# Linear attention and two feed-forward layers on one core: blocks of 512, 512, 256, 512, 512 tokens in the later passes, with one buffer for x's split

## The chip, the cores and the metric

One core of a Trainium2 chip runs the whole program. The metric is the device time of one execution in microseconds (us). The engines are called as in the profile: PE is TensorE (PEld its weight loads), DVE is VectorE, ACT is ScalarE, POOL is GpSimd, SP the engine that issues the DMAs. A matmul streams the columns of one operand through another that a weight load has put in place before; "width" below is the number of streamed columns.

## What is computed

The reference, cut to what matters (4 x 576 = 2304 tokens, 8 heads of 64, model width 512, inner width 2048, all float32):

```python
def _attn_ref(q, k, v):                       # softmax of q over its 64, of k over the 576 tokens
    kv = np.einsum('bhsd,bhse->bhde', k_s, v)
    return np.einsum('bhsd,bhde->bhse', q_s, kv)
def _moe_ref(x, w_in, w_out):                 # first layer: SiLU
    h = x @ w_in
    return (h * (1.0 / (1.0 + np.exp(-h)))) @ w_out
def _moe2_ref(x, w_in, w_out):                # second layer: Mish
    h = x @ w_in
    return (h * np.tanh(log1p(exp(h)))) @ w_out
out = _moe2_ref(_moe_ref(attention as 2304 x 512))
```

## The kernel before

**Passes, blocks, chunks.** The inner width of 2048 is cut into 16 chunks of 128. Each layer is done in two passes of 8 chunks, since the weights of 8 chunks (pool `wres`) are what is kept at a time; `passes` (L124) has four of them, two of the SiLU layer and two of the Mish layer. A pass goes over the 2304 tokens in six blocks of 384 (`BLK`, `NB`). For a block and a chunk there are two products: G1 (`ev_g1`, L645) multiplies the chunk's 512 x 128 piece of w_in by x, 12 matmuls; the activation, and a split of its result into a rounded part and a rest, give g; G2 (`ev_g2`, L664) multiplies g by the chunk's piece of w_out and adds to four banks of PSUM over the 8 chunks. Float32 accuracy comes from three products of rounded parts and rests (w, x and g each lie as two float32r parts), which is why G1 has 4 x 3 matmuls. In the SiLU layer w is the loaded and g the streamed operand of G2: 12 matmuls as wide as the block. In the Mish layer g is loaded, 128 tokens at a time, and w is streamed, 512 columns: 9 matmuls for a block of 384, however the tokens are cut three for each 128.

**What sets the order.** The list `events` (L125) has for each block X, then G1 of chunks 0 to 3, G2 of chunk 0, G1 of chunk 4, G2 of chunk 1 and so on (`SKEW` = 3 chunks apart), G2 of the last four chunks, and E. X (`ev_x`, L635) makes x's two parts, four copies on ACT and four subtractions on DVE into the tile `xs`; E (`ev_e`, L681) moves the sums out of PSUM. The first pass also carries the attention; in it a scheduler places the steps by priority. Once attention and the first weights are done, in the last-but-one block of the first pass, the loop at L745 closes the pools of the first part, opens others in their place (L746 to L752), and from there on each engine issues in the order in which the code is written (`InOrder`, L34; such instructions have line L49 in the profile, the others L47). From then on X is written `X_LEAD` = 7 events ahead of its place (L756) and a second buffer for `xs` alternates with the first (L638). If the switch happens with fewer than 7 events to go, X is written at its own place, behind E.

**Weights.** For each piece a DMA brings 64-bit words into a staging tile `st` (three of them after the switch), `w_take` and `w_join` decode them into `wt`, `w_high` and `w_low` split that into the two parts of `w`. `w_plan` (L216) sets the places in `events` where this is done. The DMA for the piece three further on waits until the join has read its staging tile.

Of the kernel before, what the change touches and what calls it, by code (L numbers as in the profile page):

```python
# [55 lines left out]
def attention_silu_mish(ctx: ExitStack, tc: tile.TileContext, q, k, v, w_in1, w_out1, w_in2, w_out2, out):  # L56
# [14 lines left out]

    BLK = 384
    NB = NT // BLK
    NT2 = BLK // P
    HALF = NCH // 2

    PARTS = (((0, HALF), (HALF, NCH)),) * 2
# [2 lines left out]


    X_LEAD, W_LEAD, T_LAG, P_LAG, A_END = 7, 8.0, 3.0, 4.0, 8.0


    W_EVERY, W_WAIT = 4.0, 8
# [11 lines left out]
    const = ctx.enter_context(tc.tile_pool(name="const", bufs=1))  # L97
    wres = ctx.enter_context(tc.tile_pool(name="wres", bufs=HALF))
    xp = ctx.enter_context(tc.tile_pool(name="xp", bufs=1))
    gp = ctx.enter_context(tc.tile_pool(name="gp", bufs=2))  # L100
    gr = ctx.enter_context(tc.tile_pool(name="gr", bufs=SKEW + 1))
    pp = ctx.enter_context(tc.tile_pool(name="pp", bufs=1, space=PSUM))

    ident = const.tile([P, P], F32, name="ident")
# [17 lines left out]


    passes = [(L, c0, c1) for L in range(2) for c0, c1 in PARTS[L]]  # L124
    events, need = [], []  # L125
    for p, (L, c0, c1) in enumerate(passes):
        cs = list(range(c0, c1))
        pend = []
        for j in range(NB):
            events.append(("X", p, j, 0))  # L130
            for c in cs:
                events.append(("G1", p, j, c))
                pend.append(("G2", p, j, c))
                if len(pend) > SKEW:
                    events.append(pend.pop(0))
            events.extend(pend)
            pend = []
            events.append(("E", p, j, 0))
        need += [e for e in events if e[0] in ("G1", "G2") and e[1] == p and e[2] == 0]
# [76 lines left out]
    def w_plan(start):  # L216
        first_mish = next(i for i, e in enumerate(events) if e[1] == len(PARTS[0]))
        ends, taken, split = [], start, 0.0
        for n in range(N0, len(need)):
            kind, p, _, c = need[n]  # L220
            last = max(i for i, e in enumerate(events) if e == (kind, p - 1, NB - 1, c - HALF if c >= HALF else c + HALF))
            if n % N0 == 0:
                taken = max(taken, nat[("X", p - 1, 1, 0)])
            b = max(taken, ends[-W_WAIT] + 0.5 if len(ends) >= W_WAIT else 0.0)
            taken = b + (W_EVERY if b < last - 8 else 2.0)
            s = max(last + 0.5, b + 2.0, split + 1.0)
            split = s
            ends.append(s + 1.0)
            assert s + 3.0 < nat[need[n]], (n, s, nat[need[n]])
            signed = b < first_mish - 1  # L230
            box = {}
            for k, f in ((b, w_take), (b + 1.0, w_join), (s, w_high), (s + 1.0, w_low)):
                todo.setdefault(int(k), []).append((k, f, n, signed, box))
# [32 lines left out]


    l1 = ExitStack()
    pools["st"] = l1.enter_context(tc.tile_pool(name="wst", bufs=4))
    pools["tm"] = l1.enter_context(tc.tile_pool(name="wtm", bufs=3))  # L270
    qp_ = l1.enter_context(tc.tile_pool(name="qp", bufs=4))
# [214 lines left out]
    def attn_start():  # L486

        n = BLK
        rn = n // P
        kt, qt, va = {}, {}, {}  # L490
        for hp in range(NP):
            kt[hp] = load_k(0, hp)
        for hp in range(NP):
            qt[hp] = load_q(0, 0, hp, 0, P, rn)
        for hp in range(NP):
            va[hp] = load_v(0, hp)
        xs[(0, 0)] = x = xp.tile([P, KC, 2, BLK], F32R, tag="xs", name="xs")
        qn = [room(P, 2 * rn * D) for _ in range(NP)]
        st = {}

        def step(what, hp):
            def do(f, *args):
                st[what, hp] = f(*args)

            def got(what):
                return st[what, hp]

            if what == "A":
                do(kT_turn, kt[hp])
            elif what == "M":  # L510
                do(kT_max, got("A"))
            elif what == "B":
                do(kT_exp, got("A"), got("M"), hp)
            elif what == "Z":
                do(kT_sum, got("B")[1])
            elif what == "K":
                do(ke_turn, got("B")[0])
            elif what == "C":
                do(ke_copy, got("K"), kt[hp])
            elif what == "D":  # L520
                do(kv_prod, kt[hp], va[hp])
            elif what == "F":
                kvs[(0, hp)] = kv_scale(got("D"), got("Z"))
            elif what == "Q":
                do(q_max, qt[hp])
            elif what == "S":
                do(q_sub, qt[hp], got("Q"))
            elif what == "E":
                do(q_exp, qt[hp])
            elif what == "R":  # L530
                do(q_sum, qt[hp])
            elif what == "N":
                do(q_norm, qt[hp], got("R"), qn[hp])
            elif what == "T":
                do(q_turn, got("N"))
            elif what == "U":
                do(q_copy, got("T"), later(xa, hp, BLK, P, BLK))
            elif what == "X":
                do(x_prod, got("U"), kvs[(0, hp)])
            elif what == "H":  # L540
                S.copy(tokens(x[:, hp, 0], rn), queries(got("X"), rn))
            elif what == "L":
                V.tensor_tensor(
                    out=tokens(x[:, hp, 1], rn), in0=queries(got("X"), rn), in1=tokens(x[:, hp, 0].bitcast(F32), rn), op=ALU.subtract
                )
            elif what == "P":
                warm_up(hp)
            elif what == "Y":
                InOrder.on = False
                tc.cur_priority += 1000  # L550
                S.copy(tokens(xaT[:, hp, :BLK], rn), queries(got("X"), rn))
                InOrder.on = True

        InOrder.on = True
        for i, o in enumerate(START):
            tc.cur_priority = 400 + 10 * i
            step(o[0], int(o[1]))
        InOrder.on = False
# [75 lines left out]

    def ev_x(p, j):  # L635
        src = xaT if passes[p][0] == 0 else xbT
        ts = slice(j * BLK, (j + 1) * BLK)
        pool = pools["xs"] if "xs" in pools and j % 2 else xp  # L638
        t = pool.tile([P, KC, 2, BLK], F32R, tag="xs", name="xs")
        for kc in range(KC):  # L640
            S.copy(t[:, kc, 0], src[:, kc, ts])
            V.tensor_tensor(out=t[:, kc, 1], in0=src[:, kc, ts], in1=t[:, kc, 0].bitcast(F32), op=ALU.subtract)
# [2 lines left out]
    def ev_g1(p, j, c):  # L645
        L = passes[p][0]
        w = w_get("G1", p, c)
        x = xs[(p, j)]
        h = banks("h1", (4, 5) if L == 0 else (4, 5, 6, 7))[:, :BLK]

        steps = [(kc, i) for i in range(3) for kc in range(KC)]
        if (p, j) == (0, 0) and c < 2:
# [1 line left out]
        for n, (kc, i) in enumerate(steps):  # L654
            s = slice(kc * P, (kc + 1) * P)
            T.matmul(h, w[:, i // 2, s], x[:, kc, i % 2], start=(n == 0), stop=(n == len(steps) - 1))
        g = gr.tile([P, 2, BLK], F32R, tag="g", name="g")
        gf = gp.tile([P, BLK], F32, tag="gf", name="gf")
        S.activation(out=gf, in_=h, func=ACTF.Silu if L == 0 else ACTF.Mish)
        V.tensor_copy(g[:, 0], gf)  # L660
        V.tensor_tensor(out=g[:, 1], in0=gf, in1=g[:, 0].bitcast(F32), op=ALU.subtract)
# [2 lines left out]
    def ev_g2(p, j, c, tiles=None):  # L664
# [1 line left out]
        w = w_get("G2", p, c)  # L666
        g = gt[(p, j, c)]
        if c == c0:
            acc[(p, j)] = [banks("acc", (0, 1, 2, 3)) for _ in range(KC if L == 0 else NT2)]
        st, sp = (c == c0), (c == c1 - 1)  # L670
        for n, (iw, ig) in enumerate(((0, 0), (0, 1), (1, 0))):
            for i, a in enumerate(acc[(p, j)]):
# [1 line left out]
                    continue  # L674
                s = slice(i * P, (i + 1) * P)
                if L == 0:
                    T.matmul(a[:, :BLK], w[:, iw, s], g[:, ig], start=st and n == 0, stop=sp and n == 2)
                else:
                    T.matmul(a, g[:, ig, s], w[:, iw], start=st and n == 0, stop=sp and n == 2)

    def ev_e(p, j, tiles=None):  # L681
        L, c0, c1 = passes[p]
        for i, a in enumerate(acc[(p, j)]):
            if tiles is not None and i not in tiles:
                continue
            if L == 0:
                y = xbT[:, i, j * BLK:(j + 1) * BLK]
                if c0:
                    V.tensor_tensor(out=y, in0=a[:, :BLK], in1=y, op=ALU.add)
                elif i % 2:  # L690
                    V.tensor_copy(y, a[:, :BLK])
                else:
                    S.copy(y, a[:, :BLK])
            else:
                it = j * NT2 + i
                o = xaO[:, it]
                if c0:
                    V.tensor_tensor(out=o, in0=a, in1=o, op=ALU.add)
# [44 lines left out]
            order.pop(0)  # L743

    for i, (what, p, j, c) in enumerate(events):  # L745
        if "xs" not in pools and state["dec"] == N0 and not order and i >= xat[1] + PACE[1] * steps["rest"] + A_END:  # L746
            w_late()
            l1.close()
            for nm, nb in (("st", 3), ("tm", W_WAIT), ("xs", 1)):
                pools[nm] = ctx.enter_context(tc.tile_pool(name="l" + nm, bufs=nb, reuse_waits="tile"))  # L750
            w_plan(i + 0.5)
            InOrder.on = True  # L752
        for k, f, *args in sorted(todo.pop(i - 1, []), key=lambda a: a[0]):
            at(k)
            f(*args)
        if InOrder.on and i + X_LEAD < len(events) and events[i + X_LEAD][0] == "X":  # L756
            at(i)
            ev_x(*events[i + X_LEAD][1:3])
        if what == "X":
            if p == 0:  # L760
                while order and order[0] <= j:
# [6 lines left out]
        if i >= len(events) - SKEW - 2:  # L768
            if what == "G2":
                tail.append(c)  # L770
                continue
            for n in range(NT2):
                for c in tail:
                    ev_g2(p, j, c, (n,))
                ev_e(p, j, (n,))
# [41 lines left out]
```

## Time and profile before

| | |
|---|---|
| median of 3 runs | 887.65 us (887.1 to 887.94) |
| profiled execution, its own time | 888.09 us |
| its span in the trace | 886.3 us |
| granted TensorE clock, mean | 0.999 |
| PE busy | 869.8 us, 98% |
| DVE busy | 444.6 us, 50% |
| ACT busy | 303.1 us, 34% |

The span is the time from the first to the last instruction of the program in the trace; 1.8 us of the execution lie around it. Busy times of matmuls overlap, since a matmul starts before the one ahead of it has ended; the time a stream of matmuls takes is read from the starts. "1.76 ... x4" means that four instructions in a row took 1.76 us together. The granted clock is a share of 2.4 GHz.

### The profile page before, as it was taken

The numbers are of one execution on the slowest core, as the hardware profiler recorded it, in microseconds if no ns is written. First come the engines' busy times: TensorE is split into PE (matmuls) and PEld (weight loads), VectorE is DVE, ScalarE is ACT, GpSimd is POOL, SyncE is SP. The second block draws the span as 40 slices with busy tenths as digits, with TensorE's granted clock in tenths as the row PEclk, the third lists the DMA queues.
The fourth block names the chain that finished last, engine by engine and source line by source line (L and its number), as shares of the span: only waits on it lengthen the run. The fifth ranks groups of instructions, "written<-read, shape, count | busy, mean of one in ns | idle before, by whom it ended". The sixth has DMA issues, their size and how long they took to land.

```text
span 886.3 us, 12434 instructions
## 1 busy us (share of the span) xinstructions
PE 869.8 (98%) x5002; PEld 810.4 (91%) x5002; DVE 444.6 (50%) x965; ACT 303.1 (34%) x592; POOL 54.0 (6%) x82
## 2 busy tenths in 40 slices
PE   7899999999999999999999999999999999999998
PEld 6688988999989999999999998998998998998997
DVE  5999366762366634523358435522349433333332
ACT  5987254563245412211235222312245211211210
POOL 3145011231000000000000000000000000000000
PEclk9999999999999999999999999999999999999999
DMA  9996211310044312200004011200002000000000
GB/s 233 248 241 131 65 36 36 72 37 1 3 140 143 96 48 64 60 21 1 1 25 143 25 47 55 65 24 1 1 24 95 1 36 37 1 36 36 1 36 36
DMA packets 61913, 53.23 MB, mean 60 GB/s; under 512 B 30368, under 2 KB 55456, under 8 KB 61856
## 3 DMA queue, kind: packets, MB, share of 16 engines
q1 hardware_dynamic: 61856, 52.44, 21.4%
q8 instruction: 39, 0.64, 0.3%
q14 instruction: 18, 0.15, 0.1%
HBM read 47.71 MB, written 4.72 MB: 59 GB/s over the span
## 4 chain that ended last, share of the span: by engine, by line
PE 72%; DVE 0%; ACT 0%; issue 0%
PE psum L49 72%; DVE xa L49 0%; ACT xs L49 0%
## 5 line engine op out<-in xcount | busy, mean ns | idle before, releaser
L49 PE MATMUL psum<-xs,w 128*128 128x384 f32 x1836 | 336.5, 335 | 0.9 <-ACT xs L49 0.8
L49 PEld LDWEIGHTS psum<-xs,w 128*128 128x128 f32 x1836 | 321.9, 188 | 7.4 <-ACT xs L49 1.8
L49 ACT ACTIVATE gf<-psum 128x384 f32<-128x384 f32 x153 | 74.9, 490 | 405.4 <-PE psum L49 316.2
L49 PE MATMUL psum<-w,g 128*128 128x512 f32 x864 | 208.0, 392 | 0.0
L49 PEld LDWEIGHTS psum<-w,g 128*128 128x128 f32 x864 | 161.3, 188 | 31.0
L49 DVE CAST g<-gf 128x384 fp32r<-128x384 f32 x153 | 55.0, 359 | 242.8 <-ACT gf L49 242.7
L49 PE MATMUL psum<-g,w 128*128 128x384 f32 x720 | 130.6, 334 | 0.0
L49 PEld LDWEIGHTS psum<-g,w 128*128 128x128 f32 x720 | 125.3, 188 | 0.0
L47 PE MATMUL psum<-xs,w 128*128 128x384 f32 x468 | 98.3, 350 | 3.0 <-ACT gf L47 1.9
L49 DVE TENSOR_TENSOR g<-gf,g 128x384 fp32r<-128x384 f32 x153 | 85.5, 559 | 5.3
L47 PEld LDWEIGHTS psum<-xs,w 128*128 128x128 f32 x468 | 80.2, 189 | 7.2 <-ACT gf L47 2.8
L47 PE MATMUL psum<-g,w 128*128 128x384 f32 x432 | 84.8, 343 | 1.2 <-DVE g L47 1.2
L47 PEld LDWEIGHTS psum<-g,w 128*128 128x128 f32 x432 | 74.7, 188 | 2.6 <-DVE g L47 1.7
L49 ACT CAST w<-wt 128x512 fp32r<-128x512 f32 x48 | 29.6, 617 | 20.9 <-DVE wt L49 15.4
L47 DVE CAST g<-gf 128x384 fp32r<-128x384 f32 x39 | 16.3, 419 | 38.8 <-ACT gf L47 38.5
L47 ACT ACTIVATE gf<-psum 128x384 f32<-128x384 f32 x39 | 18.9, 490 | 41.0 <-PE psum L47 36.9
L49 DVE TENSOR_TENSOR w<-wt,w 128x512 fp32r<-128x512 f32 x48 | 32.6, 685 | 0.6 <-ACT w L49 0.3
L49 ACT ACTIVATE wt<-st 128x512 f32<-128x512 f32 x48 | 31.8, 672 | 0.0
L49 DVE TENSOR_TENSOR xa<-psum,xa 128x512 f32<-128x512 f32 x18 | 11.5, 686 | 36.4 <-PE psum L49 36.4
L47 ACT ACT_TABLE_LOAD x22 | 28.2, 1283 | 4.3 <-PE psum L47 2.3
L49 DVE TENSOR_TENSOR xb<-psum,xb 128x384 f32<-128x384 f32 x24 | 11.7, 550 | 30.6 <-PE psum L49 30.6
L47 DVE TENSOR_TENSOR g<-gf,g 128x384 fp32r<-128x384 f32 x39 | 25.0, 641 | 1.0
(108 smaller groups left out, 561.1 us busy)
## 6 DMA issues: line engine op xcount, KB each, us to landing
st<-in_moe_w_in_dram SPq DMA_DIRECT2D x32, 512.0 KB, 3.9
st<-in_moe_w_out_dram SPq DMA_DIRECT2D x32, 512.0 KB, 3.5
out_dram<-xa SPq DMA_DIRECT2D x18, 256.0 KB, 2.1
xb<-in_k_dram SPq DMA_DIRECT2D x16, 144.0 KB, 3.4
xb<-in_v_dram SPq DMA_DIRECT2D x8, 288.0 KB, 6.8
xa<-in_k_dram SPq DMA_DIRECT2D x16, 144.0 KB, 6.2
xb<-in_v_dram SPq DMA_DIRECT2D x16, 144.0 KB, 3.6
qt<-in_q_dram SPq DMA_DIRECT2D x8, 192.0 KB, 3.3
```

The costliest lines, as they stand in the source:

```text
L47: return call(*args, **kwargs)
L49: self.last = call(*args, **kwargs)
```

## The change

The first pass keeps its six blocks of 384. The three others get five blocks, 512, 512, 256, 512 and 512 tokens wide (`WIDE`), each with its own tile sizes. There is one buffer for `xs` at a time, in a pool of its own that is closed and opened again at the switch, as are now those of `g` and `gf`, and X is written `X_NEAR` = 5 events ahead of its place, which is right behind the last G1 of the block before. The core of the diff:

```diff
-    NT2 = BLK // P
+    NARROW = [(j * BLK, BLK) for j in range(NB)]
+    WIDE = [(0, 512), (512, 512), (1024, 256), (1280, 512), (1792, 512)]
...
+    X_NEAR = SKEW + 2
...
-    gp = ctx.enter_context(tc.tile_pool(name="gp", bufs=2))
-    gr = ctx.enter_context(tc.tile_pool(name="gr", bufs=SKEW + 1))
...
+    blocks = [NARROW] + [WIDE] * (len(passes) - 1)
...
-        for j in range(NB):
+        for j in range(len(blocks[p])):
...
+    pools["xs"] = l1.enter_context(tc.tile_pool(name="xs", bufs=1))
+    pools["gf"] = l1.enter_context(tc.tile_pool(name="gp", bufs=2))
+    pools["g"] = l1.enter_context(tc.tile_pool(name="gr", bufs=SKEW + 1))
...
-        ts = slice(j * BLK, (j + 1) * BLK)
-        pool = pools["xs"] if "xs" in pools and j % 2 else xp
-        t = pool.tile([P, KC, 2, BLK], F32R, tag="xs", name="xs")
+        t0, n = blocks[p][j]
+        ts = slice(t0, t0 + n)
+        t = pools["xs"].tile([P, KC, 2, n], F32R, tag="xs", name="xs")
...
-        h = banks("h1", (4, 5) if L == 0 else (4, 5, 6, 7))[:, :BLK]
+        h = banks("h1", (4, 5) if L == 0 else (4, 5, 6, 7))[:, :blocks[p][j][1]]
...
-            acc[(p, j)] = [banks("acc", (0, 1, 2, 3)) for _ in range(KC if L == 0 else NT2)]
+            acc[(p, j)] = [banks("acc", (0, 1, 2, 3)) for _ in range(KC if L == 0 else blocks[p][j][1] // P)]
...
-        if "xs" not in pools and state["dec"] == N0 and not order and i >= xat[1] + PACE[1] * steps["rest"] + A_END:
+        if not InOrder.on and state["dec"] == N0 and not order and i >= xat[1] + PACE[1] * steps["rest"] + A_END:
...
-            for nm, nb in (("st", 3), ("tm", W_WAIT), ("xs", 1)):
+            for nm, nb in (("xs", 1), ("gf", 2), ("g", SKEW + 1), ("st", 3), ("tm", W_WAIT)):
...
-        if InOrder.on and i + X_LEAD < len(events) and events[i + X_LEAD][0] == "X":
+        if InOrder.on and i + X_NEAR < len(events) and events[i + X_NEAR][0] == "X":
             at(i)
-            ev_x(*events[i + X_LEAD][1:3])
+            ev_x(*events[i + X_NEAR][1:3])
```

What it does to the order, at three places. First PE, from the end of the first pass into the second (`xs,w` is G1, `g,w` is G2 of the SiLU layer; the size is 128 rows by the width). Before:

```order
L49 MATMUL psum<-g,w 128x384 x48
L49 MATMUL psum<-xs,w 128x384 x48
L49 MATMUL psum<-g,w 128x384 x12
L49 MATMUL psum<-xs,w 128x384 x12
L49 MATMUL psum<-g,w 128x384 x12
```

and with the change, there and at the third block:

```order
L49 MATMUL psum<-g,w 128x384 x48
L49 MATMUL psum<-xs,w 128x512 x48
L49 MATMUL psum<-g,w 128x512 x12
L49 MATMUL psum<-xs,w 128x512 x12
...
L49 MATMUL psum<-g,w 128x512 x48
L49 MATMUL psum<-xs,w 128x256 x48
L49 MATMUL psum<-g,w 128x256 x12
```

The runs have as many matmuls as before, of other widths, and a pass has five blocks of them in place of six.

Second ACT, at the switch to the written order, in the last-but-one block of the first pass (`gf` is the activation's result of the last chunk, `wt<-st` a weight's decode, `xb<-psum` two of E's copies, `xs<-xa` X's copies; the names in brackets are the engines or DMA queues waited for). Before:

```order
L49 ACTIVATE gf<-psum 128x384 [waits DVE_49,PE_49,Activation_49]
L49 ACTIVATE wt<-st 128x512
L49 ACTIVATE wt<-st 128x512 [waits Pool_49] x2
L49 COPY xb<-psum 128x384 [waits PE_49] x2
L49 CAST xs<-xa 128x384 x4
L49 ACTIVATE wt<-st 128x512 [waits DMAHW3_49]
L49 ACTIVATE gf<-psum 128x384 [waits DVE_49,PE_49,Activation_49]
```

and with the change:

```order
L49 ACTIVATE gf<-psum 128x384 [waits PE_49]
L49 ACTIVATE wt<-st 128x512 [waits Pool_49]
L49 CAST xs<-xa 128x384 x4
L49 ACTIVATE wt<-st 128x512 x2
L49 COPY xb<-psum 128x384 [waits PE_49] x2
L49 ACTIVATE wt<-st 128x512 [waits DMAHW3_49]
L49 ACTIVATE gf<-psum 128x384 [waits PE_49]
```

X's four copies stand ahead of E's copies now. Third DVE at the same place. Before:

```order
L49 CAST g<-gf 128x384 [waits Activation_49]
L49 TENSOR_TENSOR g<-gf,g 128x384 [waits DVE_49]
L49 TENSOR_SCALAR st<-st 128x512
L49 SCALAR_TENSOR_TENSOR wt<-wt,st 128x512 [waits DVE_49,Activation_49]
L49 TENSOR_SCALAR st<-st 128x512
L49 SCALAR_TENSOR_TENSOR wt<-wt,st 128x512 [waits DVE_49,Activation_49]
L49 TENSOR_SCALAR st<-st 128x512
L49 COPY xb<-psum 128x384 [waits PE_49]
L49 COPY xb<-psum 128x384 [waits DMAHW6_49,PE_49]
L49 SCALAR_TENSOR_TENSOR wt<-wt,st 128x512 [waits DVE_49,Activation_49]
L49 TENSOR_TENSOR xs<-xa,xs 128x384 [waits Activation_49] x4
```

and with the change:

```order
L49 CAST g<-gf 128x384 [waits DVE_49,PE_49,Activation_49]
L49 TENSOR_TENSOR g<-gf,g 128x384 [waits DVE_49]
L49 TENSOR_SCALAR st<-st 128x512
L49 TENSOR_TENSOR xs<-xa,xs 128x384 [waits Activation_49] x4
L49 SCALAR_TENSOR_TENSOR wt<-wt,st 128x512 [waits DVE_49,Pool_49]
L49 TENSOR_SCALAR st<-st 128x512
L49 SCALAR_TENSOR_TENSOR wt<-wt,st 128x512 [waits DVE_49,Activation_49]
```

The four subtractions of X stand ahead of the first join (`wt<-wt,st`). The cast at the top waits for PE now: its tile `g` is the first of the new pool, whose address (177696 to 180768 in a partition) overlaps that of the old pool's last tile (178720 to 181792), which G2 of the chunk before it reads.

## Rows read from the trace of the kernel before

**Rows 1.** The page: busy time by engine, share of the span, instructions.
```profile
PE 869.8 (98%) x5002; PEld 810.4 (91%) x5002; DVE 444.6 (50%) x965; ACT 303.1 (34%) x592; POOL 54.0 (6%) x82
```
**Rows 2.** Passes two to four: us; PE, PEld, DVE, ACT, POOL busy (count); clock; DMA.
```profile
283.22:482.90 199.68, 199.68 (x1153) 199.68 (x1153) 96.87 (x202) 56.02 (x114) 0.00 (x0) 1.00 0.16 51
482.90:682.64 199.74, 199.74 (x1010) 181.64 (x1009) 94.58 (x189) 55.86 (x113) 0.00 (x0) 1.00 0.13 40
682.64:882.37 199.73, 199.73 (x1009) 181.47 (x1007) 70.48 (x144) 35.37 (x75) 0.00 (x0) 1.00 0.06 23
```
**Rows 3.** PE in order of time, second pass: start us, us, line, operation, count.
```profile
339.38 2.24 PE L49 MATMUL psum<-xs,w 128*128 128x384 f32 x12
341.46 8.48 PE L49 MATMUL psum<-g,w 128*128 128x384 f32 x48
349.78 2.41 PE L49 MATMUL psum<-xs,w 128*128 128x384 f32 x13
```
**Rows 4.** PE in order of time, third pass, widths alternating.
```profile
557.81 2.24 PE L49 MATMUL psum<-w,g 128*128 128x512 f32 x9
559.89 2.27 PE L49 MATMUL psum<-xs,w 128*128 128x384 f32 x12
562.00 2.24 PE L49 MATMUL psum<-w,g 128*128 128x512 f32 x9
```
**Rows 5.** PE in order of time, inside a run of 36 matmuls of 512 columns.
```profile
576.41 6.51 PE L49 MATMUL psum<-w,g 128*128 128x512 f32 x28
```
**Rows 6.** In order of time, first pass: two loads after a wait; three transposes.
```profile
29.94 0.30 PEld L47 LDWEIGHTS psum<-xs,w 128*128 128x128 f32 x2 [0.62 <-ACT xs L49]
143.50 0.49 PE L47 MATMUL psum<-ident,qn 128*128 128x128 f32 x3
```
**Rows 7.** Groups by shape: line engine op, out<-in, xcount | busy us, mean ns.
```profile
L49 PEld LDWEIGHTS psum<-xs,w 128*128 128x128 f32 x1836 | 321.9, 188 | 7.4 <-ACT xs L49 1.8 <-DVE xs L49 0.5
L49 PE MATMUL psum<-w,g 128*128 128x512 f32 x864 | 208.0, 392 | 0.0
L49 DVE TENSOR_TENSOR w<-wt,w 128x512 fp32r<-128x512 f32 x48 | 32.6, 685 | 0.6 <-ACT w L49 0.3
L47 PE MATMUL psum<-ident,qn 128*128 128x128 f32 x36 | 6.1, 273 | 0.2 <-ACT qT L47 0.2
```
**Rows 8.** In order of time, the hand-over to the written order (239 to 258 us).
```profile
239.32 8.48 PE L49 MATMUL psum<-g,w 128*128 128x384 f32 x48
239.57 0.49 ACT L49 ACTIVATE gf<-psum 128x384 f32<-128x384 f32 x1 [3.67 <-PE psum L49]
239.96 1.80 ACT L49 ACTIVATE wt<-st 128x512 f32<-128x512 f32 x3
240.09 0.36 DVE L49 CAST g<-gf 128x384 fp32r<-128x384 f32 x1 [3.21 <-ACT gf L49]
240.49 0.56 DVE L49 TENSOR_TENSOR g<-gf,g 128x384 fp32r<-128x384 f32 x1
240.96 0.42 DVE L49 TENSOR_SCALAR st<-st 128x512 uint32<-128x512 uint32 x1
241.49 0.69 DVE L49 SCALAR_TENSOR_TENSOR wt<-wt,st 128x512 uint32<-128x512 uint32 x1
...
242.21 0.37 SPq L154 DMA_DIRECT2D st<-in_moe_w_in_dram  x1
...
247.32 0.86 ACT L49 COPY xb<-psum 128x384 f32<-128x384 f32 x2 [5.57 <-PE psum L49]
...
248.07 1.76 ACT L49 CAST xs<-xa 128x384 fp32r<-128x384 f32 x4
...
249.03 1.96 DVE L49 TENSOR_TENSOR xs<-xa,xs 128x384 fp32r<-128x384 f32 x4
...
258.26 2.24 PE L49 MATMUL psum<-g,w 128*128 128x384 f32 x12
```
**Rows 9.** The page: DMA issues, KB each, median us to landing.
```profile
st<-in_moe_w_in_dram SPq DMA_DIRECT2D x32, 512.0 KB, 3.9
```

More of the change, by code (lines that the diff above doesn't have):

```diff
@@ L220, in w_plan @@
             kind, p, _, c = need[n]
-            last = max(i for i, e in enumerate(events) if e == (kind, p - 1, NB - 1, c - HALF if c >= HALF else c + HALF))
+            last = max(i for i, e in enumerate(events) if e == (kind, p - 1, len(blocks[p - 1]) - 1, c - HALF if c >= HALF else c + HALF))
             if n % N0 == 0:
@@ L496, in attn_start @@
             va[hp] = load_v(0, hp)
-        xs[(0, 0)] = x = xp.tile([P, KC, 2, BLK], F32R, tag="xs", name="xs")
+        xs[(0, 0)] = x = pools["xs"].tile([P, KC, 2, BLK], F32R, tag="xs", name="xs")
         qn = [room(P, 2 * rn * D) for _ in range(NP)]
@@ L656, in ev_g1 @@
             T.matmul(h, w[:, i // 2, s], x[:, kc, i % 2], start=(n == 0), stop=(n == len(steps) - 1))
-        g = gr.tile([P, 2, BLK], F32R, tag="g", name="g")
-        gf = gp.tile([P, BLK], F32, tag="gf", name="gf")
+        n = blocks[p][j][1]
+        g = pools["g"].tile([P, 2, n], F32R, tag="g", name="g")
+        gf = pools["gf"].tile([P, n], F32, tag="gf", name="gf")
         S.activation(out=gf, in_=h, func=ACTF.Silu if L == 0 else ACTF.Mish)
@@ L676, in ev_g2 @@
                 if L == 0:
-                    T.matmul(a[:, :BLK], w[:, iw, s], g[:, ig], start=st and n == 0, stop=sp and n == 2)
+                    T.matmul(a[:, :blocks[p][j][1]], w[:, iw, s], g[:, ig], start=st and n == 0, stop=sp and n == 2)
                 else:
@@ L682, in ev_e @@
         L, c0, c1 = passes[p]
+        t0, n = blocks[p][j]
         for i, a in enumerate(acc[(p, j)]):
@@ L685, in ev_e @@
                 continue
+            a = a[:, :n] if L == 0 else a
             if L == 0:
-                y = xbT[:, i, j * BLK:(j + 1) * BLK]
+                y = xbT[:, i, t0:t0 + n]
                 if c0:
-                    V.tensor_tensor(out=y, in0=a[:, :BLK], in1=y, op=ALU.add)
+                    V.tensor_tensor(out=y, in0=a, in1=y, op=ALU.add)
                 elif i % 2:
-                    V.tensor_copy(y, a[:, :BLK])
+                    V.tensor_copy(y, a)
                 else:
-                    S.copy(y, a[:, :BLK])
+                    S.copy(y, a)
             else:
-                it = j * NT2 + i
+                it = t0 // P + i
                 o = xaO[:, it]
@@ L771, in attention_silu_mish @@
                 continue
-            for n in range(NT2):
+            for n in range(blocks[p][j][1] // P):
                 for c in tail:
```

## Prediction

> **What bounds the kernel now.** I read the busy shares first: TensorE (PE) 98% of the span [rows 1]. Matmuls overlap in the records, so that share does not say how fast they follow each other, and the next view is the stretches by pass, to be read for TensorE's idle time and clock: passes two, three and four take 199.68, 199.74 and 199.73 us, in none is TensorE idle, and the granted clock is 1.00, the 2.4 GHz level [rows 2]. VectorE is busy under 49% there and ScalarE under 29%. So 599 us of the span are a stream of matmuls with no hole in it, and the question is what one matmul takes from start to start, by its width.
>
> Spacing of starts, from the order in time. 384 columns: 48 matmuls from 341.46 to 349.78, 8.32 us, **173.3 ns** each [rows 3]. 512 columns: 28 matmuls last 6.51 us; less the last one's 0.39 that is 6.12 over 27, **226.7 ns** [rows 5, 7]. 128 columns more cost 53.4 ns, 0.417 ns a column; 384 columns are then 160.0 ns and 512 are 213.3, and each matmul has **13.3 ns on top that do not depend on its width**. That is what wider blocks save.
>
> A second thing shows only in the Mish layer, where 384-wide and 512-wide runs alternate: from 557.81 to 562.00, nine and twelve matmuls take 4.19 us [rows 4], against 9 x 226.7 + 12 x 173.3 = 4.12. Inside a long run of one width it is gone [rows 5]. In the SiLU layer, where both kinds have 384 columns, twelve take 2.08 us, exactly 12 x 173.3 [rows 3]. A block has five such pairs: 5 x 0.067 = 0.33 us. I read it as a price of changing the width.
>
> **The change, part by part.** All sums are in the profiled execution: span 886.3, its own time 888.09, which is 0.44 above the median 887.65.
>
> *Second pass.* Before, 192 matmuls a block in six blocks, 1152 x 173.3 = 199.7. After, four blocks of 512 (768 matmuls x 226.7 = 174.1) and one of 256 (192). What a 256-wide one takes, no row shows. Lower bound: 256 x 0.417 + 13.3 = 120 ns. The weight load under it could hold it up: a load that nothing covers puts its successor's start 0.30 - 0.19 = 0.11 us later [rows 6, 7], so loads can follow each other at 110 ns; with the same 13.3 that is 123. The nearest row of a stream this short: three 128-column fp32 transposes, each with its own 128-column load, in 0.49 us; less the last's 0.273, 108 ns apart [rows 6, 7]. There the load hides. I take **123**, between the bounds of 120 and, from above, 173.3 (as if the load, not the width, paced it). 192 x 123 = 23.6; the pass takes 197.7, **-2.0 us**.
>
> What a weight load costs is where the Trainium skill speaks against the change. "TensorE: Matmul & The Clock Gate", section LDWEIGHTS, gives a load as its columns over 1.2, an estimate of 107 ns for 128 columns: as long as the 107 ns that 256 columns stream, so no slack is left. Rows 6 agree with the size (110), and whether it hides in full no row here shows.
>
> *Third and fourth pass.* Only the first product changes width: 576 matmuls of 384 become 384 of 512 and 96 of 256. 384 x 226.7 + 96 x 123 + 432 x 226.7 = 87.0 + 11.8 + 97.9 = 196.8; four blocks now have one width throughout and pay no switches, the 256 block pays 0.33: 197.1 against 199.74, **-2.6 us each**.
>
> The same page, section Back-to-back issue gap, gives columns over 2.4 plus 2.5 ns: 162.5 for 384. The trace has 173.3, and the measurement decides. By the page's 2.5 the 384 matmuls saved would be worth 1 us in place of five.
>
> *The hand-over in the last-but-one block of the first pass.* Here the order moves. Now, TensorE loses 2.3 us: the 48 second-product matmuls start at 239.32, 96 x 0.1733 later is 255.96, and the next second product starts at 258.26 [rows 8]. It waits for x's split, which stands behind the eviction copies (247.32) on ScalarE and behind a weight step on VectorE. The change puts the split ahead of both, so those waits go. What is late next, from the order of the changed program:
> - The last chunk's g now comes from the new pool, whose place overlaps the tile that the second product just before it reads. Its cast waits for that product's end, 245.56, plus the 0.25 us that the activation at 239.57 took to follow the matmuls' end at 239.32 [rows 8]; with 0.36 for the cast and 0.06 to TensorE, that stalls 0.67, and 0.1 for a load that nothing covers: 0.8 us.
> - Behind that cast on VectorE stand its partner, a shift, the four subtractions of the split (1.96 us [rows 8]) and only then the join (0.69) that frees a staging buffer for the next weight DMA. By the spacings of the same steps now, from the cast's start [rows 8]: 245.81 + 0.40 + 0.47 + 0.42 + 1.96 + 0.6 = 249.7 for the join's end, where now the DMA is issued at 242.21. It lands 3.9 us after issue [rows 9], at 253.6. ScalarE has a decode that waits for it ahead of the first activation of the block; 0.6 for the decode (three take 1.80) and 0.49 for the activation [rows 8], and that ends near 254.6. The first layer has two PSUM banks for this product, so TensorE does two chunks (248.4 to 252.6) and waits 2.1 us for the third.
> Together 2.9 in place of 2.3: **+0.6 us**. Bounds: 0.8 if the DMA is in time (-1.5), and 1.5 us more if it lands later.
>
> *One buffer for x.* The split may start when the last first product of a block has ended and must be done before the next block starts, four second products later: 48 x 226.7 = 10.9 us, after the 256 block 48 x 123 = 5.9 (Mish layer 24 x 226.7 = 5.4). Work there after a 256 block: 0.25 lag, 0.4 activation (0.49 at 384 [rows 8], less a bit), four casts (1.76 at 384 [rows 8], 2.3 at 512), a last subtraction of 0.69 [rows 7]: 3.6 us. It fits, with 1.8 to spare; with a weight's decode and join between (0.6 and 0.69 [rows 8]) it still does. Cost zero.
>
> *The rest.* Fewer, longer activations and evictions on half-idle engines, covered by the stream; weights are planned by places in the order, which last longer in wide blocks; in the 256 block a chunk lasts 2.9 us, and VectorE has in it g's cast and subtraction (0.36 and 0.56 at 384, less a third), half a weight's 0.42 + 0.69 + 0.69, and an eighth of four evictions and four subtractions of 0.69: 2.2 us [rows 7, 8]. The tail after the last matmul is unchanged: four row blocks instead of three, the last one's add and DMA alone exposed. Zero.
>
> Sum: -2.0 - 2.6 - 2.6 + 0.6 = **-6.6**: 881.5 on the profiled execution, 881.0 on the median.
>
> **The rivals.**
> 1. *The weight load paces the 256-wide matmuls* (slower). For: 110 ns of load under 107 of stream; no row has this stream at full rate with so little room. Against: the transposes' 108 ns. There are 192 + 96 + 96 = 384 such matmuls; the gain of 6.6 is gone when each takes 6.6/384 = 17 ns more, 140. At 173.3 it costs 384 x 50 = 19.3: 900.3. At load plus stream, 217, it costs 36. Chance 0.14 of ending slower, 0.04 of ending within the noise; a little over 123 is in my own range.
> 2. *The 0.067 us belong to the change of operands* (w streamed, g loaded), not of width. Then the eight wide blocks pay 0.33 each: +2.6, 883.6. Against: the SiLU layer changes its streamed operand too and shows nothing; for: there the loaded operand stays w. Chance 0.20.
> 3. *x's split is late after the 256 blocks*, by the 2 us that a late split costs now [rows 8], three times: +6, 887. Against: the 1.8 us to spare. Chance 0.06.
> 4. *Nothing per matmul to save*: excluded by two widths on one line, but for 0.02.
> My forecast as worked out: 0.54. It and rival 2 end faster.
>
> **How the numbers follow.** 0.2% is 1.8 us, about what a measurement tells from no change. Faster (under 885.9): 0.54 + 0.20 + half of rival 3 = 0.77; within: 0.04 + 0.03 + 0.02 = 0.09; slower: 0.14. The low end takes 120 for 123 (-1.2) and a DMA in time (-1.5): 878.3, so 878. The high end takes rival 2, rival 3 and the first part of rival 1: 888.5.
>
> **What would show it.** Twelve matmuls of 512 in the second pass take 2.72 us, of 256 1.44 to 1.48; the passes take 197.7, 197.1, 197.1; in wide Mish blocks nine or twelve matmuls show no excess; between 246 and 258 two stalls of 0.8 and 2.1. Rival 1 shows as 256-wide runs of twelve over 1.7 us, rival 2 as 4.19-like pairs in equal widths, rival 3 as idle TensorE behind xs. A pass longer than 199.7 would make the forecast wrong.

## The result

The changed kernel takes 880.6 us (median of 5 runs, 879.92 to 880.86) against 887.94 us (887.1 to 889.18) for the kernel before on the same chip: ratio 0.9915, 95% interval 0.9901 to 0.993. That is 7.3 us less; 6.6 were forecast. The profiled execution, the fastest of the five, spans 878.1 us against 886.3: 8.2 less, since it lies 0.7 us under its median and the profiled one of before 0.2 above.

The page's busy times, the counterpart of [rows 1]:

```profile
PE 860.3 (98%) x4618; PEld 744.0 (85%) x4618; DVE 437.2 (50%) x904; ACT 296.7 (34%) x553; POOL 54.4 (6%) x82
```

TensorE is as busy as before, with 384 matmuls fewer. The stretches of passes two, three and four, as in [rows 2] (us; PE, PEld, DVE, ACT, POOL busy; clock; DMA):

```profile
283.86:481.04 197.18, 197.18 (x962) 167.26 (x962) 93.68 (x179) 55.79 (x104) 0.00 (x0) 1.00 0.17 55
481.04:677.62 196.58, 196.58 (x914) 164.75 (x913) 94.57 (x173) 53.91 (x100) 0.00 (x0) 1.00 0.13 40
677.62:874.20 196.58, 196.58 (x913) 164.58 (x911) 66.50 (x123) 32.00 (x61) 0.00 (x0) 1.00 0.06 23
```

Again no idle time and the full clock: -2.50, -3.16 and -3.15 us. What a matmul takes, from PE in order of time: two 256-wide rows of the second pass, two wide blocks of the Mish layer, and its 256 block (answering to [rows 3 to 5]).

```profile
388.21 5.92 PE L49 MATMUL psum<-g,w 128*128 128x256 f32 x48
393.97 2.23 PE L49 MATMUL psum<-xs,w 128*128 128x512 f32 x9
...
535.43 2.88 PE L49 MATMUL psum<-w,g 128*128 128x512 f32 x12
538.15 2.88 PE L49 MATMUL psum<-xs,w 128*128 128x512 f32 x12
540.88 2.88 PE L49 MATMUL psum<-w,g 128*128 128x512 f32 x12
...
568.08 5.92 PE L49 MATMUL psum<-xs,w 128*128 128x256 f32 x48
...
585.11 5.63 PE L49 MATMUL psum<-w,g 128*128 128x512 f32 x24
590.58 1.75 PE L49 MATMUL psum<-xs,w 128*128 128x512 f32 x7
```

256 columns: 5.76 us for 48, **120.0 ns**. 512 columns: 2.72 us for twelve, 226.7 ns, also where the two products alternate. The Mish 256 block lasts 22.50 us from 568.08 to 590.58; 96 x 0.12 + 48 x 0.2267 is 22.40, so its changes of width cost 0.10.

The hand-over, in order of time (answering to [rows 8]):

```profile
239.36 6.41 PE L49 MATMUL psum<-g,w 128*128 128x384 f32 x36
241.64 0.49 ACT L49 ACTIVATE gf<-psum 128x384 f32<-128x384 f32 x1 [5.70 <-PE psum L49]
...
245.86 0.36 DVE L49 CAST g<-gf 128x384 fp32r<-128x384 f32 x1 [8.94 <-PE psum L49]
...
246.27 2.36 PE L49 MATMUL psum<-g,w 128*128 128x384 f32 x12 [0.51 <-DVE g L49]
...
247.06 1.96 DVE L49 TENSOR_TENSOR xs<-xa,xs 128x384 fp32r<-128x384 f32 x4
...
249.69 0.37 SPq L156 DMA_DIRECT2D st<-in_moe_w_in_dram  x1
...
253.53 0.68 ACT L49 ACTIVATE wt<-st 128x512 f32<-128x512 f32 x1 [4.51 <-DMA st<-in_moe_w_in_dram]
...
254.63 4.43 PE L49 MATMUL psum<-xs,w 128*128 128x384 f32 x24 [1.83 <-ACT gf L49]
...
258.89 2.24 PE L49 MATMUL psum<-g,w 128*128 128x384 f32 x12
```

The cast's input is there at 242.1 and it starts at 245.86; the DMA goes out at 249.69, 7.5 us later than before; TensorE waits twice. By 0.1733 a matmul, the 36 from 239.36 end at 245.60 and the next starts at 246.27, the twelve from there end at 248.35 and the next starts at 248.47: 0.67 + 0.12. The 24 from 248.47 end at 252.63, the next starts at 254.63; those 24 end at 258.79, the next starts at 258.89: 2.0 + 0.10. From 239.36 to the second pass at 283.86 are 44.50 us; before, from 239.32 to 283.22, 43.90.

The profiled gain in stages: hand-over +0.60, passes -2.50 - 3.16 - 3.15, and 0.01 from the start and the tail: -8.2, the whole difference of the spans. Of the 8.8 in the passes, 5.1 are the 384 matmuls saved at 13.3 ns; the other 3.7 go with changes of width in the Mish layer that are no longer made (experiment 4 has their price).

### The profile page after: what moved, and what is told of

The parts are those of the page before. It is cut to its first block, busy times and chain, and to the rows that moved or that the text cites. A ratio compares the mean times of both kernels' runs of the same rounds, so it can differ in the third digit from the quotient of the medians.

```text
span 878.1 us, 11558 instructions
## 1 busy us (share of the span) xinstructions
PE 860.3 (98%) x4618; PEld 744.0 (85%) x4618; DVE 437.2 (50%) x904; ACT 296.7 (34%) x553; POOL 54.4 (6%) x82
## 4 chain that ended last, share of the span: by engine, by line
PE 89%; DVE 5%; ACT 1%; DMA 1%; issue 1%; ACTq 0%; DVEq 0%; SPq 0%
PE psum L49 72%; PE psum L47 17%; DMA st<-in_moe_w_out_dram 1%; DVE g L47 1%; DVE qz L47 1%; DVE kmx L47 1%; DVE w L47 0%; DMA st<-in_moe_w_in_dram 0%; ACT xa L47 0%; DVE st L47 0%; DVE wt L47 0%; DVE xs L47 0%; DVE qmx L47 0%; DVE xs L49 0%; ACT xs L49 0%
## 5 line engine op out<-in xcount | busy, mean ns | idle before, releaser
L49 PE MATMUL psum<-xs,w 128*128 128x512 f32 (+2 forms) x1548 | 327.9, 366 | 1.8 <-ACT gf L49 1.8
L49 ACT ACTIVATE gf<-psum 128x512 f32<-128x512 f32 (+2 forms) x129 | 71.0, 550 | 407.5 <-PE psum L49 292.1
L49 DVE CAST g<-gf 128x512 fp32r<-128x512 f32 (+2 forms) x129 | 51.3, 397 | 277.0 <-ACT gf L49 267.8
L49 PE MATMUL psum<-g,w 128*128 128x512 f32 (+2 forms) x624 | 128.8, 361 | 0.5 <-DVE g L49 0.5
L47 PE MATMUL psum<-xs,w 128*128 128x384 f32 x468 | 98.4, 350 | 2.9 <-ACT gf L47 2.1
L47 PE MATMUL psum<-g,w 128*128 128x384 f32 x432 | 84.7, 343 | 1.3 <-DVE g L47 1.3
L49 DVE TENSOR_TENSOR g<-gf,g 128x512 fp32r<-128x512 f32 (+2 forms) x129 | 81.7, 633 | 4.4
L47 DVE CAST g<-gf 128x384 fp32r<-128x384 f32 x39 | 16.1, 413 | 38.9 <-ACT gf L47 38.6
L47 ACT ACTIVATE gf<-psum 128x384 f32<-128x384 f32 x39 | 18.9, 490 | 40.9 <-PE psum L47 36.9
L47 DVE TENSOR_TENSOR g<-gf,g 128x384 fp32r<-128x384 f32 x39 | 25.1, 644 | 1.0
```

What stands on the lines that cost most here:

```text
L47: return call(*args, **kwargs)
L49: self.last = call(*args, **kwargs)
```

## Experiments

All runs start from the changed kernel. Since executions differ by up to 3.5 us ahead of the hand-over (its 48 second products start between 238.6 and 242.2 in these profiles, where the programs are still alike), I compare stretches after that point, and medians as ratios to the kernel before on the same chip.

**1. The order and the pools alone.**

```diff
-    WIDE = [(0, 512), (512, 512), (1024, 256), (1280, 512), (1792, 512)]
+    WIDE = NARROW
```

> The change with the later passes cut into six blocks of 384 as before; what is left of it is the single buffer for x's split, the pools of g and gf opened again at the switch, and X written nearer to its place. My theory (the width gives the gain, the new order costs 0.6 us once): TensorE's three later passes take 199.7 us each as before, the hand-over keeps the two stalls of 0.8 and 2.1 us in place of one of 2.3, and the median is about 888.5 us, 0.6 above the kernel before. Rival (the gain comes from the order and the pools, the widths only go along): about 881 us, passes of 197.

Measured: 885.29 us, ratio 0.9965 (0.9953 to 0.9978); neither number. The passes as stretches, and under them the hand-over in order of time:

```profile
281.15:480.83 199.68, 199.68 (x1154) 199.68 (x1154) 96.41 (x201) 55.71 (x113) 0.00 (x0) 1.00 0.16 51
480.83:680.56 199.73, 199.73 (x1009) 181.64 (x1009) 94.66 (x189) 56.88 (x113) 0.00 (x0) 1.00 0.13 42
680.56:880.28 199.72, 199.72 (x1009) 181.47 (x1007) 70.78 (x145) 35.42 (x75) 0.00 (x0) 1.00 0.06 23
```

```profile
239.55 8.48 PE L49 MATMUL psum<-g,w 128*128 128x384 f32 x48
...
241.89 0.36 DVE L49 CAST g<-gf 128x384 fp32r<-128x384 f32 x1 [4.79 <-PE psum L49]
...
247.87 8.48 PE L49 MATMUL psum<-xs,w 128*128 128x384 f32 x48
...
256.19 2.24 PE L49 MATMUL psum<-g,w 128*128 128x384 f32 x12
```

The passes are those of before to 0.01 us: the gain in them is the width's alone. But the hand-over has no stall at all (239.55 to 281.15 is 41.60 us, 240 x 0.1733). So the new order by itself saves the whole 2.3 us that TensorE lost there before, and in the changed kernel the 2.9 us of new stalls take them back. The narrower tiles of x and gf had moved the first new g tile to 172576. The old tile there is read by the first twelve second products only, which end at 241.63, and the cast goes at 241.89. My expectation had overlooked that the widths set the addresses.

**2. The address alone, twice.** The kernel of experiment 1, with the g tile put back to the address of the changed one by padding a tile in memory: first x's, then gf's.

```diff
-        t = pools["xs"].tile([P, KC, 2, n], F32R, tag="xs", name="xs")
+        t = pools["xs"].tile([P, KC, 2, 544 if InOrder.on else n], F32R, tag="xs", name="xs")[:, :, :, :n]
```

> The kernel of e1 (six blocks of 384 in every pass, the new order and pools) with one edit: the tile of x's split is made 544 columns wide in memory after the switch, of which 384 are used, so that the first new g tile lies at 177696 to 180768 as in the changed kernel, over the old tile that the second product ahead reads; in e1 it lies at 172576 to 175648. Nothing else differs. My theory (the address alone decides the hand-over): the cast of the last chunk's g waits to 245.6 or later, the stalls of 0.8 and 2.1 us are back, the second pass starts near 283.9, the median is 2.7 to 2.9 us above that of e1, about 888.1 us. Rival (the wider blocks, not the address, cause the stalls): as e1, 885.3 us.

```diff
-        gf = pools["gf"].tile([P, n], F32, tag="gf", name="gf")
+        gf = pools["gf"].tile([P, 1024 if InOrder.on else n], F32, tag="gf", name="gf")[:, :n]
```

> As e7, but the padding is put elsewhere, since the padded x tile slowed the first products by itself (173.3 ns became 174.6 on average): after the switch the tile of gf, which no matmul reads, is 1024 columns wide in memory, of which 384 are used. The first new g tile lies at 177696 to 180768 again, and x's split has the layout of e1. My theory (the address alone decides the hand-over): from the start of the 48 second products to the start of the second pass 44.35 us as in e7, against 41.60 in e1; the three later passes 199.7 us each as in e1; the median 2.75 us above e1's, about 888.0 us. Rival (the padding of x caused part of the stalls): below 887 us.

Measured: 889.63 us, 1.0026 (1.0015 to 1.0036), and 889.58 us, 1.0011 (1.0 to 1.0021). The second one's hand-over in order of time, and its second pass as a stretch:

```profile
240.15 6.41 PE L49 MATMUL psum<-g,w 128*128 128x384 f32 x36
...
246.66 0.36 DVE L49 CAST g<-gf 128x384 fp32r<-128x384 f32 x1 [8.95 <-PE psum L49]
...
250.49 0.37 SPq L156 DMA_DIRECT2D st<-in_moe_w_in_dram  x1
...
254.08 0.67 ACT L49 ACTIVATE wt<-st 128x512 f32<-128x512 f32 x1 [4.25 <-DMA st<-in_moe_w_in_dram]
...
255.19 4.45 PE L49 MATMUL psum<-xs,w 128*128 128x384 f32 x24 [1.57 <-ACT gf L49]
```

```profile
284.44:484.12 199.68, 199.68 (x1154) 199.68 (x1153) 96.46 (x201) 55.78 (x113) 0.00 (x0) 1.00 0.16 51
```

Both stalls are back, in blocks of 384: 240.15 to 284.44 is 44.29 us, 2.69 more than in experiment 1, and the passes are unchanged. In the first padding it is 2.75 (239.09 to 283.44). The address decides the hand-over. By the ratios the second padding and experiment 1 lie 0.46% apart, some 4.1 us and more than the 2.7; the two intervals leave room for 2.0 to 6.0, and 0.6 of the rest lies ahead of the hand-over in the profiles. The remainder is not placed. Padding x also slowed the first products; that is told at the end.

**3. The pool of g opened ahead of that of gf**, in the changed kernel. The first new g tile then lies at 173600, over the old tile that the first twelve second products read and a part of one that nobody reads any more; it is not a place that has been free for long, as my expectation had it, but one that is free 24 second products earlier than in the changed kernel.

```diff
-            for nm, nb in (("xs", 1), ("gf", 2), ("g", SKEW + 1), ("st", 3), ("tm", W_WAIT)):
+            for nm, nb in (("xs", 1), ("g", SKEW + 1), ("gf", 2), ("st", 3), ("tm", W_WAIT)):
```

> The changed kernel with one edit: at the switch the pool of g is opened ahead of that of gf, so that the first new g tile lies on a place that has been free for long. My theory (the cast of the last chunk's g waits for the second product that reads the old tile under it, and this cast holds up VectorE's queue, the join, the weight DMA and so ScalarE's activation): both stalls of the hand-over (0.8 and 2.1 us) vanish, the second pass starts near 281.0 instead of 283.9, the median is about 877.7 us. Rival (the weight DMA is late whatever the cast does): only the 0.8 goes, about 879.8 us. Rival (the waits stand in E and X, as before): no change, 880.6 us.

Measured: **877.48 us**, 0.9885 (0.9872 to 0.9898), the fastest kernel here; its interval lies below that of the change. The hand-over:

```profile
239.03 8.48 PE L49 MATMUL psum<-g,w 128*128 128x384 f32 x48
...
241.37 0.36 DVE L49 CAST g<-gf 128x384 fp32r<-128x384 f32 x1 [4.78 <-PE psum L49]
...
245.20 0.37 SPq L156 DMA_DIRECT2D st<-in_moe_w_in_dram  x1
...
247.35 8.48 PE L49 MATMUL psum<-xs,w 128*128 128x384 f32 x48
...
248.98 0.69 ACT L49 ACTIVATE wt<-st 128x512 f32<-128x512 f32 x1 [1.09 <-DMA st<-in_moe_w_in_dram]
...
255.67 2.24 PE L49 MATMUL psum<-g,w 128*128 128x384 f32 x12
```

Counted from the first second product, the cast runs 4.2 us earlier than in the changed kernel (2.34 us after it, not 6.50), the DMA as much (6.17, not 10.33), and TensorE never waits: 239.03 to 280.63, where the second pass starts, is 41.60. Both stalls hang on this one cast.

**4. A pair of 384 in place of 512 and 256.**

```diff
-    WIDE = [(0, 512), (512, 512), (1024, 256), (1280, 512), (1792, 512)]
+    WIDE = [(0, 512), (512, 512), (1024, 384), (1408, 384), (1792, 512)]
```

> The changed kernel with blocks of 512, 512, 384, 384, 512 tokens: as many matmuls and as many columns, none of 256. My theory (each matmul costs its columns at 0.417 ns plus 13.3 ns whatever the width; changing the width costs 0.33 us a block of 384 in the Mish layer, and 0.10 for the block of 256): the second pass stays at 197.2 us, the third and fourth get 2 x 0.33 in place of 0.10, +0.56 each, about 881.7 us. Rival (256 columns hide the weight load badly, so that a pair of 384 is cheaper): second pass below 197.2 and a median under 880 us.

Measured: 882.26 us, 0.9939 (0.9926 to 0.9953), and the passes:

```profile
285.33:482.55 197.22, 197.22 (x961) 174.73 (x961) 93.67 (x179) 55.80 (x104) 0.00 (x0) 1.00 0.17 55
482.55:679.70 197.15, 197.15 (x913) 168.70 (x912) 94.02 (x172) 54.38 (x100) 0.00 (x0) 1.00 0.12 40
679.70:876.90 197.20, 197.20 (x913) 168.51 (x911) 66.43 (x123) 31.89 (x61) 0.00 (x0) 1.00 0.06 23
```

Second pass +0.04, the Mish passes +0.57 and +0.62 where 0.56 was expected: with equal counts of matmuls and columns only the width changes in the Mish layer cost.

**5. Nine blocks of 256.**

```diff
-    WIDE = [(0, 512), (512, 512), (1024, 256), (1280, 512), (1792, 512)]
+    WIDE = [(i * 256, 256) for i in range(9)]
```

> The changed kernel with nine blocks of 256 in each of the later passes. My theory (13.3 ns for every matmul whatever its width): 768 more matmuls in the second pass and 384 more in the third and the fourth, 1536 x 13.3 ns = 20.5 us, and eight more blocks per Mish pass with 0.1 us of width changes, 1.6: about 902.6 us, and 256-wide starts 120 ns apart. Rival (time goes by columns, the gain came from something else): about 881 us. Rival (VectorE and ScalarE do not keep up when all blocks are narrow, since x's split, the weights and the evictions have less cover): over 905 us, with TensorE idle behind g, w or xs.

Measured: 909.17 us, 1.0246 (1.023 to 1.0262). By the profile the second pass takes 208.18 us, 1728 x 0.12 = 207.36 and 0.82 around one wait for an activation in its first block. The last two take 414.5 (491.94 to 906.43, the last matmul's start and 0.227), where 2 x 196.58 plus 768 x 0.0133 and 1.6 are 405.0. The 9.5 over it lie around the start of the fourth pass, most of them here, in four stretches. (The profiled execution is the slowest of the four, 3.0 us over their median, so the others lose less.)

```profile
698.00:702.84 4.84, 4.84 (x41) 4.80 (x41) 4.56 (x9) 1.68 (x3) 0.00 (x0) 1.00 0.18 74
702.84:706.81 3.97, 0.16 (x2) 0.00 (x0) 3.78 (x8) 1.69 (x4) 0.00 (x0) 0.92 0.00 0
706.81:712.90 6.09, 6.09 (x20) 5.37 (x21) 3.08 (x9) 1.72 (x5) 0.00 (x0) 0.50 0.01 3
712.90:720.00 7.10, 7.10 (x45) 6.35 (x44) 2.06 (x6) 0.77 (x2) 0.00 (x0) 0.99 0.00 0
```

VectorE is busy for 3.78 of the 3.97 us in which TensorE has all but nothing to do; in the order in time it works through weights and evictions ahead of the cast that TensorE waits for. The next 6.09 us run at half the clock, some 3 us lost, and shorter waits from 693.5 to 698 are the rest. So in this execution the theory's 20.5 us are there, and the rival on VectorE is right for the rest, at that place. (The hand-over has no stall here; the tiles lie elsewhere again.)

**6. Two blocks of 128.**

```diff
-    WIDE = [(0, 512), (512, 512), (1024, 256), (1280, 512), (1792, 512)]
+    WIDE = [(0, 512), (512, 512), (1024, 128), (1152, 128), (1280, 512), (1792, 512)]
```

> The changed kernel with the block of 256 cut into two of 128. My theory (13.3 ns a matmul on top of its columns, as long as the weight load hides): 128 columns take 66.7 ns, 192 more matmuls in the second pass and 96 more in the others are 5.1 us, and x's split is late after a block of 128, whose last four second products last 3.2 us, by some 0.7 us twice a pass in the second and more in the others: about 887 to 890 us. Rival (below some width the load sets the pace, 110 ns as in the exposed loads): 128-wide starts 110 ns apart, 768 x 43 ns = 33 us more, about 920 us.

Measured: 919.66 us, 1.0357 (1.0338 to 1.0376). My theory fell, the rival was right:

```profile
386.11 5.52 PE L49 MATMUL psum<-g,w 128*128 128x128 f32 x48
391.47 1.73 PE L49 MATMUL psum<-xs,w 128*128 128x128 f32 x14
```

48 matmuls in 5.36 us, 111.7 ns each and not 66.7. That is within 2 ns of the 110 ns at which loads with nothing to cover them follow each other, so I read it as the load's pace; no run streams 128 columns without a load for each matmul, so a cost of narrow streams as such is not excluded. The price accounts for the whole time: 768 x 111.7 in place of 384 x 120.0 ns are 39.7 us, and by the ratios the kernel is 39.2 slower than the changed one. A matmul of 256 columns, at 120.0, is only 8 ns longer than one of 128; by the spacings at 256, 384 and 512 a stream of (111.7 - 13.3) / 0.417 = 236 columns would be as long as its load, an estimate that stands on that reading.

**7. Two matmuls in a row with one loaded operand**, in the Mish layer's second product.

```diff
+        kinds = ((0, 0), (0, 1), (1, 0)) if L == 0 else ((0, 0), (1, 0), (0, 1))
+        pairs = [(n, i) for n in range(3) for i in range(len(acc[(p, j)]))]
+        if L == 1:
+            pairs.sort(key=lambda x: (x[0] == 2, x[1], x[0]))
```

> The changed kernel with the nine-matmul groups of the Mish layer's second product in another order, in which two matmuls in a row use the same part of g as their loaded operand and write the same PSUM bank. If the 13.3 ns that every matmul has on top of its columns belong to the change of the loaded operand (or to the change of the bank), one matmul in three of those is without it: 2 x 432 matmuls of the second product a third of them, 288 x 13.3 ns = 3.8 us less, about 876.8 us. If they belong to every matmul: no change, 880.6 us, with the 512-wide starts 226.7 ns apart throughout.

Measured: 880.0 us, 0.9913 (0.99 to 0.9925), and the run of second products at the end of a block:

```profile
557.45 11.04 PE L49 MATMUL psum<-w,g 128*128 128x512 f32 x48
568.33 1.36 PE L49 MATMUL psum<-xs,w 128*128 128x256 f32 x10
```

10.88 us for 48, 226.7 ns as ever. That the operand or the bank changes is not what the 13.3 ns pay for. The kernel still issues a load for each matmul, so whether they belong to the load stays open.

## Why the prediction was right

- **13.3 ns a matmul, whatever its width**: held. 256 columns, not in the trace of before, take 120.0 ns = 106.7 + 13.3, and experiment 5 finds 768 matmuls more in the second pass at that price, but for one stall. Experiment 1 has the passes of before to 0.01 us when the widths are put back, so that rival 4 is out. The second pass, with 192 matmuls fewer and no width change inside a block, is 2.50 us shorter; 192 x 13.3 ns are 2.56. By the 2.5 ns that the Trainium skill ("TensorE: Matmul & The Clock Gate", Back-to-back issue gap) adds to the columns for the gap of a matmul by itself, that would be an estimated 0.5 us; the measurement decides.
- **The 256-wide price**, taken as 123 between 120 and 173.3: it was the lower bound. 192 x 3 ns are 0.6 us of the second pass (-2.5 for -2.0) and 96 x 3 ns 0.3 of each Mish pass.
- **Rival 1, the load paces the 256-wide matmuls**: fell, by a small margin. Experiment 6 has 128-wide matmuls at 111.7 ns, read as the load's pace. At 120.0 the 256-wide matmul is longer than that, and load and stream did not add. The prediction's support from the transposes was weak: their 108 ns, read there as a load that hides, lie nearer to this 111.7 than to the 66.7 that 128 columns and 13.3 ns would take, so that row speaks for a load's pace more than for a hidden load. The estimate of 107 ns for a load by the Trainium skill ("TensorE: Matmul & The Clock Gate", LDWEIGHTS) is 5 ns below the spacing of experiment 6.
- **Width changes**, 0.33 us for a block: right for 384 beside 512 (experiment 4), too much for 256 beside 512, where it is 0.10. That is the other 0.23 us of each Mish pass. Rival 2, that the excess belongs to the change of operands, fell: equal widths alternate at 2.72 us for twelve.
- **The hand-over**, +0.6: measured +0.60, with the two stalls at their places (0.67 + 0.12 for 0.8, 2.0 + 0.10 for 2.1). The steps came where the chain had put them: the DMA goes out at 249.69 (249.7 forecast) and TensorE goes on at 254.63 (254.6). The chain from the cast to the join, the DMA and the activation is shown by experiments 2 and 3. The premise that the first new tile lies over the one that the product just ahead reads carries all 2.9 us: in experiments 1 and 3, where the tile lies elsewhere, TensorE never waits.
- **One buffer for x**, 0 with 1.8 us to spare: held. The split after the 256 block of the second and of the third pass:

```profile
388.74 2.17 ACT L49 CAST xs<-xa 128x512 fp32r<-128x512 f32 x4
...
389.55 2.49 DVE L49 TENSOR_TENSOR xs<-xa,xs 128x512 fp32r<-128x512 f32 x4
...
585.64 2.17 ACT L49 CAST xs<-xb 128x512 fp32r<-128x512 f32 x4
...
586.45 2.49 DVE L49 TENSOR_TENSOR xs<-xb,xs 128x512 fp32r<-128x512 f32 x4
```

It is done at 392.04 and at 588.94, and the next block starts at 393.97 and 590.58: 1.9 and 1.6 us to spare. Rival 3 fell.

The mis-sized terms are the 256-wide price (1.15 us over 384 matmuls) and the width change (0.23 twice): together the 1.6 us between the forecast 6.6 and the profiled 8.2.

## What to carry to other kernels

Where a stream of matmuls has no hole, read the spacing at two widths: what is left over per matmul times the matmuls saved is what wider blocks give, as long as the narrowest width is no slower than that rule (256 kept to it here, 128 did not). Where two widths alternate, look at the pairs too: equal widths gave 3.7 us here beside the 5.1 of the matmuls saved. When pools are closed and opened again amid a stream, look at which old tile lies under the first new one and who reads it last: the wait lands on an in-order queue and delays all behind it, and opening the pools in another order removed it (2.9 us in the stages, 2.7 by the ratios).

## What the hardware showed beside that

- **The 13.3 ns are gone at the lower clock level**, in the one stretch where it was seen. In experiment 5, after 3.97 us almost without work, the granted clock is 0.50 (1.2 GHz) from 706.81 to 712.90:

```profile
709.54 2.76 PE L49 MATMUL psum<-xs,w 128*128 128x256 f32 x12
712.10 1.95 PE L49 MATMUL psum<-w,g 128*128 128x512 f32 x6
```

Twelve 256-wide matmuls take 2.56 us, 213.3 ns each, which is 256 columns at 1.2 GHz with nothing on top. What the 13.3 ns at the full clock are is open.
- **Padding x's tile costs.** With x's tile 544 columns wide in memory (experiment 2, first padding), the first products take 8.38 us for 48, 174.6 ns each (in order of time), and the second pass 200.32 us in place of 199.68 (the stretch under it):

```profile
283.44 8.53 PE L49 MATMUL psum<-xs,w 128*128 128x384 f32 x48
291.82 0.51 PE L49 MATMUL psum<-g,w 128*128 128x384 f32 x2
```

```profile
283.44:483.76 200.32, 200.32 (x1153) 200.32 (x1153) 96.52 (x201) 55.77 (x113) 0.00 (x0) 1.00 0.16 51
```

With gf's tile padded instead and the same place for g, the second pass stays at 199.68, so it is x's tile. Why is not settled: the stride between x's parts and the places where they lie change together, and no run takes them apart.
